# Attention further ahead of its product, factor tails on VectorE, factors made in place, borders reordered

## The chip, the cores and the metric

The kernel runs on one core of a Trainium2 chip. The metric is the device time of one execution in microseconds; runs are told by their median. The engines are TensorE (PE; its weight loads are PEld), VectorE (DVE), ScalarE (ACT), GpSimd (POOL) and SyncE (SP), which here issues every DMA. TensorE's clock has two levels, 1.2 and 2.4 GHz; the profile gives the granted share.

## The reference

Pooled attention and two MLPs on 8 x 576 = 4608 tokens, in float32. The weights come in as 64-bit floats.

```
k_p, v_p = means over 8 neighbours of k, v          # 72 keys a head; 8 batches, 8 heads, 64 dims
scores = (q @ k_p^T) / sqrt(64);  attn = exp(scores - max);  attn /= sum(attn) + 1e-9
x  = attn @ v_p                                     # as 4608 x 512
x1 = silu(x @ w_in)  @ w_out                        # 512 -> 2048 -> 512
h  = x1 @ w_in2;  out = (h * clip(h + 3, 0, 6) / 6) @ w_out2
```

## The kernel before, in words

Every float32 matmul outside the attention is made of three products of halves that TensorE reads at full rate (`F32R`): a *head*, which ScalarE rounds by a copy, and a *tail*, the rest, which another engine gets by a subtraction. The last three of the four big products also use a seven-product form of 2 x 2 blocks: seven sums of weight blocks (the *factors*, `k` = 0 to 6) and seven sums of operand blocks.

The work has four stages, each of nine groups of 512 tokens (`g`), four tiles of 128 tokens (`t`) in a group.

- *Hidden stage* (L863-939): `h_mm` makes one of sixteen slices `f` of a group's hidden values, 12 matmuls of 512 columns; a slot is `(g, f)`, 144 in all. Beside them runs the attention of the next group's tiles, by the table of `stages(g)`: `scores` into two `ps_a` banks; "soft" (`below_max` on VectorE, `exps` on ScalarE); `norm`; a transposition, in the first group on TensorE (`probs_T`), later on VectorE in 32 x 32 blocks (`vector_T`), which go to DRAM and come back in the right order (L475, L479); `weighted`, the product with v five (first group) or six slots after the scores; and `split_x`. `silu` of a slot is issued in the next one. The first group also converts the sixteen slices of w_in (`split_a`, `split_b`).
- Beside it, *factor jobs* (`run_job`) convert w_out and, for 5 of 8 pairs, w_in2: scale on ScalarE (L163), three bit operations on VectorE (L169-L176), sums of blocks on GpSimd (`combine`, L195), a head on ScalarE (`half_head`, L187) and a tail on GpSimd (`half_tail`, L191) for each of seven factors; the two are stored to DRAM (`ws`) and loaded again when the factor is wanted (`load_factor`).
- *Wide stage* (`block_stage(0, ...)`): 63 blocks (g, k) of 48 matmuls of 256 columns. Its operands are split by `split_g` (L678 on ScalarE, L679 on VectorE) one block ahead. After each block `run_steps(2)` does two steps of the last three w_in2 pairs.
- *Product stage* (L1115-1177): 252 slots of 12 matmuls of 256 columns, with gates behind them and one step a slot of the w_out2 pairs. Its operands come from x1 by `x_sum` (GpSimd), `x_head` (ScalarE) and `x_tail`.
- *Last stage* (`block_stage(1, ...)`): again 63 blocks of 48.

All instructions are issued in the order of the program (`manual_schedule`); each engine, and SP's queue of DMAs, takes its own in that order and waits at its head. DMA issues that need a result are put into `later` and issued at the top of the next slot. Tags name buffers: a tile waits until the last use of the tile that held its tag is over.

Of the kernel before, what the change touches and what calls it, by code (L numbers as in the profile page):

```python
# [10 lines left out]
F32 = mybir.dt.float32  # L11
# [14 lines left out]
def kernel(  # L26
# [154 lines left out]
    def half_b(mag, dst):  # L181

        half_tail(mag, half_head(mag), dst)

    def half_head(mag):
        t = prep_tile("out", [P, 2, HW], F32R)
# [27 lines left out]
    def pair_steps(p, piece):  # L214
# [12 lines left out]
        def head(k, key):  # L227
            def run():
                t[k] = half_head(m[key])
            return run  # L230

        def tail(k, key):
            return lambda: half_tail(m[key], t.pop(k), ws[piece][d][k][:, j])
# [13 lines left out]
    def pair_jobs(p, piece, rest):  # L247
# [4 lines left out]
        def out(k, key):  # L252
            return lambda: half_b(m[key], ws[piece][d][k][:, j])
# [22 lines left out]
    def load_factor(m, d, k, tag):  # L276
        t = wts.tile([P, 2, 2, HW], F32R, tag=tag, name="wst")
        nc.sync.dma_start(out=t.bitcast(F32), in_=ws[m][d][k])
# [76 lines left out]
    def load_q(t, tag=None):  # L355
        qt = staging(tag or f"o{10 + t % 2}", DM)
# [70 lines left out]

    def den_of(t):
# [4 lines left out]
    def norm(t, summed=0):  # L433
# [3 lines left out]
        nc.vector.tensor_reduce(out=den[:, :n], in_=pr[:, :n], op=ALU.add, axis=AX.X)  # L437
# [6 lines left out]
    def probs_T(t, tags=A, tag=None, warm=0):  # L444
        pr = p_t.pop(t)
        pT = staging(tag or f"o{12 + t % 2}", H * P)[:SP]
# [14 lines left out]
    def vector_T(t):  # L461
# [4 lines left out]
        bT = staging(f"o{14 + t % 2}", NB * H * Q).rearrange("p (j h q) -> p j h q", j=NB, h=H)  # L466
        pT = staging(f"o{12 + t % 2}", H * P)[:SP].rearrange("p (i h q) -> p i h q", h=H, q=Q)
# [117 lines left out]
    def x_sum(i):  # L585
        b11, b12, b21, b22 = x_blocks()
        if i == 1:
            combine(ALU.subtract, b11, b12, b11)
        elif i == 2:
            combine(ALU.subtract, b11, b22, b11)  # L590
        elif i == 3:
            combine(ALU.subtract, b12, b22, b12)
        elif i == 5:
            combine(ALU.subtract, b21, b21, b11)
# [16 lines left out]
    def make_x(g, i):  # L611

        x_sum(i)
# [46 lines left out]
    LAST = (0, 1, 4, 2, 5, 6, 3)  # L660
# [62 lines left out]
    def stages(g):  # L723
        d = [[] for _ in range(NF)]
        if g + 1 < NG:
            for i in range(TPG):
                t = TPG * (g + 1) + i
                s = (3, 5, 7, 9)[i] if g == 0 else (0, 2, 5, 8)[i]
                d[s].append(("scores", t))
                d[s + 1].append(("soft", t))  # L730
                d[s + 2].append(("norm", t))
                if g == 0:
                    d[s + 3].append(("probs", t))
                else:
                    d[s + 2].append(("turn", t))
                w = s + 5 if g == 0 else s + 6
                d[w].append(("weighted", t))
                d[w + 1].append(("split", t))
        return d

    with tc.manual_schedule():
# [93 lines left out]
        kv_jobs = [(b, j) for b in range(2, B) for j in range(NPAIR)]  # L835
        kv_wait = []
        BUSY = (2, 10)
# [3 lines left out]
        w_need = [(d, k) for k in LAST for d in range(ND)]  # L841
        w_tags = [f"o{i}" for i in range(12)] + [f"i{i}" for i in range(NF)]
# [20 lines left out]
        for g in range(NG):  # L863
            todo = stages(g)
            if g == NG - 1:
                while jobs or jobs_b:
                    run_job()
                    load_halves()
                early.close()
                open_ring()  # L870
            for f in range(NF):
# [6 lines left out]
                while later:  # L878
                    later.pop(0)()
                ps = h_mm(g, f)  # L880
                for what, t in todo[f]:
# [6 lines left out]
                if late_silu:  # L888
                    silu(*late_silu.pop())
                late_silu.append((g, f, ps))  # L890
                for what, t in todo[f]:
                    if what == "split":
                        split_x(t, pv.pop(t))
# [3 lines left out]
                elif g < NG - 1 and f not in BUSY:  # L897
                    run_job()
                for what, t in todo[f]:
                    if what == "soft":  # L900
                        new_pr(t)
                        below_max(t, 0)
                        below_max(t, 1)
                        exps(t, 0)
                        exps(t, 1)
                    elif what == "norm":
                        norm(t)
# [4 lines left out]
                if n < 3:  # L912
                    for j in ((0, 1), (2,), (3,))[n]:
# [3 lines left out]
                if f % 2 == 1:  # L917
                    for b, j in kv_wait:
                        pool_k(b, j, nc.gpsimd)
                        pool_v(b, j)  # L920
                    kv_wait = []
# [317 lines left out]
```

## Time and profile before

| | |
|---|---|
| median of 3 runs | 1668.45 us (1665.39 to 1670.14) |
| the profiled execution | 1662.0 us, of which the span, first to last instruction, is 1660.2 |
| PE, PEld | 1534.5 us busy (92%), 1449.6 (87%) |
| DVE, ACT, POOL | 1264.3 (76%), 737.1 (44%), 530.7 (32%) |
| mean granted clock | 0.967 |
| DMA | 350.56 MB, 211 GB/s |

Busy shares are means over stages that differ. In a row of the timeline the bracket is the idle time of the engine just before it and what ended it; in a list of groups the numbers behind the bar are busy us, the mean ns of one, and idle time.

### The profile page before, as it was taken

The page shows a single profiled execution, that of the slowest core. Times are in us where ns is not written, and L with a number is a line of the kernel's source. Part 1 is how long each engine was busy: PE and PEld are TensorE (multiplying, and loading weights), DVE is VectorE, ACT ScalarE, POOL GpSimd, SP SyncE. Part 2 cuts the span into 40 slices and gives each one's busy share as a digit, 9 for nine tenths or more (in the row PEclk, how much of TensorE's full clock was granted, in tenths as well). Part 3 has the DMA queues.
Part 4 walks back from the last instruction along what each step waited for, and adds up shares of the span by engine and source line. Part 5 has one row for each costly group of instructions (what it writes and reads, how often), then busy time and mean ns, then how long its engine had stood idle before and what let it go on. Part 6 is the DMA issues. An engine that isn't in the chain of part 4 may idle for free.

```text
span 1660.2 us, 30941 instructions
## 1 busy us (share of the span) xinstructions
PE 1534.5 (92%) x11870; PEld 1449.6 (87%) x11870; DVE 1264.3 (76%) x1674; ACT 737.1 (44%) x1241; POOL 530.7 (32%) x590
## 2 busy tenths in 40 slices
PE   7579888898889979999999979999999999999999
PEld 6468777776768869999999979999999899999998
DVE  7867688677787429999977758778776687887776
ACT  5343333333334224444433446777676543344333
POOL 5744545545543002221300036766665000000000
PEclk9789999999999998999999989999999999999999
DMA  9327777867876995554544966656567974444441
GB/s 326 108 66 231 249 235 256 274 221 242 280 244 230 338 358 176 170 184 154 172 146 145 340 252 210 223 211 204 210 215 255 358 274 130 128 151 133 154 149 45
DMA packets 188276, 350.56 MB, mean 211 GB/s; under 512 B 17504, under 2 KB 90080, under 8 KB 188128
## 3 DMA queue, kind: packets, MB, share of 16 engines
q1 hardware_dynamic: 188128, 348.59, 61.7%
q8 instruction: 93, 1.52, 0.4%
q14 instruction: 55, 0.45, 0.1%
HBM read 199.10 MB, written 149.42 MB: 210 GB/s over the span
## 4 chain that ended last, share of the span: by engine, by line
PE 65%; DVE 12%; DMA 11%; issue 4%; POOL 3%; ACT 3%; SPq 1%; DVEq 0%; ACTq 0%; POOLq 0%
PE pl L708 20%; PE pl L692 19%; PE px L630 10%; PE hps L528 6%; PE pz L630 5%; PE py L630 3%; DMA ws<-hout 2%; DMA bl<-stage 2%; DMA wst<-ws 2%; DMA g<-g 2%; DMA stage<-in_k_dram 2%; DVE hmag L176 1%; DVE g L542 1%; DVE hmag L172 1%; DVE hmag L169 1%
## 5 line engine op out<-in xcount | busy, mean ns | idle before, releaser
L528 PE MATMUL hps<-x,whl 128*128 128x512 f32 x1728 | 411.0, 397 | 7.4 <-POOL whl L138 2.8
L528 PEld LDWEIGHTS hps<-x,whl 128*128 128x128 f32 x1728 | 336.6, 198 | 64.4 <-DVE g L542 4.6
L678 ACT ACTIVATE gs<-gr 128x1024 fp32r<-128x1024 f32 x252 | 253.7, 1054 | 260.0 <-issue 104.2
L692 PE MATMUL pl<-gs,wst 128*128 128x256 f32 x3024 | 341.6, 276 | 14.2 <-ACT gs L678 13.7
L692 PEld LDWEIGHTS pl<-gs,wst 128*128 128x128 f32 x3024 | 340.9, 193 | 14.9 <-ACT gs L678 13.9
L679 DVE TENSOR_TENSOR gs<-gr,gs 128x1024 fp32r<-128x1024 f32 x252 | 303.4, 1246 | 54.4 <-ACT gs L678 54.1
L708 PE MATMUL pl<-wst,gs 128*128 128x256 f32 x3024 | 339.8, 276 | 3.3 <-ACT gs L678 2.5
L708 PEld LDWEIGHTS pl<-wst,gs 128*128 128x128 f32 x3024 | 339.5, 193 | 3.7 <-ACT gs L678 2.7
L191 POOL TENSOR_TENSOR hout<-hmag,hout 128x256 fp32r<-128x256 f32 x168 | 149.2, 895 | 417.5 <-ACT hout L187 393.2
L630 PE MATMUL px<-xst,wst 128*128 128x256 f32 x1728 | 208.2, 277 | 11.0 <-ACT c L1148 9.8
L630 PEld LDWEIGHTS px<-xst,wst 128*128 128x128 f32 x1728 | 201.4, 194 | 12.0 <-ACT c L1148 10.2
L542 DVE SCALAR_TENSOR_TENSOR g<-g,hps 128x512 f32<-128x512 f32 x144 | 96.3, 677 | 105.4 <-ACT g L541 101.4
L671 DVE TENSOR_TENSOR gr<-gr 128x1024 f32<-128x1024 f32 x144 | 176.5, 1267 | 0.0
L541 ACT ACTIVATE g<-hps 128x512 f32<-128x512 f32 x144 | 83.8, 588 | 79.5 <-PE hps L528 61.5
L630 PE MATMUL pz<-xst,wst 128*128 128x256 f32 x864 | 109.8, 276 | 2.6 <-POOL xst L607 2.5
L187 ACT ACTIVATE hout<-hmag 128x256 fp32r<-128x256 f32 x168 | 68.1, 411 | 94.2 <-POOL hmag L195 68.7
L607 POOL TENSOR_TENSOR xst<-xr,xst 128x512 fp32r<-128x512 f32 x56 | 76.8, 1371 | 93.5 <-ACT xst L602 88.7
L630 PEld LDWEIGHTS pz<-xst,wst 128*128 128x128 f32 x864 | 102.8, 192 | 3.8 <-POOL xst L607 3.3
L195 POOL TENSOR_TENSOR hmag<-hmag 128x256 f32<-128x256 f32 x96 | 92.1, 963 | 15.9 <-DVE hmag L176 12.7
L413 ACT ACTIVATE pr<-pr 128x288 f32<-128x288 f32 x64 | 28.1, 442 | 153.5 <-DVE pr L406 153.5
L195 POOL TENSOR_TENSOR xr<-xr 128x512 f32<-128x512 f32 x36 | 48.6, 1350 | 128.2 <-DVE xst L607 124.9
L169 DVE TENSOR_SCALAR hmag<-hmag 128x256 uint32<-128x256 uint32 x96 | 52.6, 548 | 40.3 <-ACT hmag L163 39.2
(81 smaller groups left out, 1533.1 us busy)
## 6 DMA issues: line engine op xcount, KB each, us to landing
gr<-g SPq DMA_DIRECT2D x144, 512.0 KB
ws<-hout SPq DMA_DIRECT2D x168, 256.0 KB
wst<-ws SPq DMA_DIRECT2D x84, 512.0 KB
g<-g SPq DMA_DIRECT2D x144, 256.0 KB
g<-go SPq DMA_DIRECT2D x144, 256.0 KB
hraw<-in_moe_w_out_dram SPq DMA_DIRECT2D x64, 256.0 KB
bl<-stage SPq DMA_DIRECT2D x28, 384.0 KB
stage<-in_k_dram SPq DMA_DIRECT2D x32, 288.0 KB
```

The lines of the kernel that those rows point to most:

```text
L191: nc.gpsimd.tensor_tensor(out=t[:, 1], in0=mag, in1=t[:, 0].bitcast(F32), op=ALU.subtract)
L195: nc.gpsimd.tensor_tensor(out=out, in0=a, in1=b, op=op)
L528: nc.tensor.matmul(ps, w[:, c, :], shuffled(x[:, c, :]), start=(c == 0 and n == 0), stop=(c == NKC - 1 and n == 2),)
L541: nc.scalar.activation(in_two(t), dealt(ps), AF.Tanh)
L542: nc.vector.scalar_tensor_tensor(out=in_two(t), in0=in_two(t), scalar=1.0, in1=dealt(ps), op0=ALU.add, op1=ALU.mult)
L607: (eng or nc.gpsimd).tensor_tensor(out=t[:, 1], in0=x_source(i), in1=t[:, 0].bitcast(F32), op=ALU.subtract)
L630: nc.tensor.matmul(ps[:, j * HW:(j + 1) * HW], w[:, j, a, c, :], shuffled(x[:, b, c, :]), start=(first and j == 0 and n == 0 and c == 0), ...
L671: nc.vector.tensor_tensor(out=to, in0=a, in1=b, op=ALU.subtract)
L678: nc.scalar.activation(t[:, dd, 0], src, AF.Copy)
L679: nc.vector.tensor_tensor(out=t[:, dd, 1], in0=src, in1=t[:, dd, 0].bitcast(F32), op=ALU.subtract)
L692: nc.tensor.matmul(ps[:, c * HW:(c + 1) * HW], w[:, b, c * P:(c + 1) * P], shuffled(t[:, dd, a, i]), start=(dd == 0 and c == 0 and i == 0 ...
L708: nc.tensor.matmul(ps[:, c * HW:(c + 1) * HW], t[:, dd, a, i, c * P:(c + 1) * P], shuffled(w[:, b]), start=(dd == 0 and c == 0 and i == 0 ...
```

## The change

- *Attention.* A tile's scores come five slots (group 1), seven (group 2) or ten (from group 3) ahead of its weighted product, by a table over all slots (`todo`, `start`). `all_exps` takes the maxima of all eight heads and then one exponential per head on ScalarE, straight from the scores' banks, which also gives the sums, so that `norm` sums nothing. q has buffers of its own; transposed probabilities have four. k and v are loaded 16 slots ahead of the first scores that read them and pooled three slots later.
- *Order in a slot.* `silu`, `split_x` and the exponentials are issued ahead of the slot's matmuls and jobs. Jobs run in the slots of a group that are not 0, 3, 6 or 13, and in the even slots of the last group.
- *Tails.* `split_b` and `half_tail` subtract on VectorE instead of GpSimd.
- *In place.* Eight of the 28 factors of w_out (`k` = 0 and 1) are made in the buffers in which the wide stage reads them (`direct`, tags o0 to o7), without a store and a load. The other twenty are loaded at another pace, the last after the first raw weights of the wide stage's steps.
- *Borders.* The wide stage's steps begin at its fifth block; the product stage's at its third column (`e > 1`), two in some slots. `x_sum` of the first operands goes to VectorE, operands 5 and 6 are made in the first five product slots, and `split_g(1, 0, 0)` is issued in the last column of products.

```diff
-        nc.gpsimd.tensor_tensor(out=t[:, 1, :], in0=mag, in1=t[:, 0, :].bitcast(F32), op=ALU.subtract)
+        nc.vector.tensor_tensor(out=t[:, 1, :], in0=mag, in1=t[:, 0, :].bitcast(F32), op=ALU.subtract)
...
+    def half_head(mag, m, d, k, j):
+        if (m, d, k) in direct:
+            if j == 0:
+                load_factor(m, d, k, direct[m, d, k], fill=False)
+            t = w_st[m, d, k][:, j]
+        else:
+            t = prep_tile("out", [P, 2, HW], F32R)
         nc.scalar.activation(t[:, 0], mag, AF.Copy)
         return t
 
-    def half_tail(mag, t, dst):
-        nc.gpsimd.tensor_tensor(out=t[:, 1], in0=mag, in1=t[:, 0].bitcast(F32), op=ALU.subtract)
-        later.append(lambda: nc.sync.dma_start(out=dst, in_=t.bitcast(F32)))
+    def half_tail(mag, t, m, d, k, j):
+        nc.vector.tensor_tensor(out=t[:, 1], in0=mag, in1=t[:, 0].bitcast(F32), op=ALU.subtract)
+        if (m, d, k) not in direct:
+            later.append(lambda: nc.sync.dma_start(out=ws[m][d][k][:, j], in_=t.bitcast(F32)))
...
+    direct = {(2, d, k): f"o{ND * i + d}" for i, k in enumerate(LAST[:2]) for d in range(ND)}
...
+    def all_exps(t):
+
+        mx = att.tile([P, H, 1], F32, tag="mxa", name="mxa")
+        for a in range(2):
+            nc.vector.tensor_reduce(
+                out=mx[:, a * NPAIR:(a + 1) * NPAIR], in_=s_t[t][a], op=ALU.max, axis=AX.X
+            )
+        nc.vector.tensor_scalar(out=mx, in0=mx, scalar1=-ESCALE, scalar2=None, op0=ALU.mult)
+        for h in range(H):
+            a, i = divmod(h, NPAIR)
+            nc.scalar.activation(
+                p_t[t][:, a, i], s_t[t][a][:, i], AF.Exp, scale=ESCALE, bias=mx[:, h],
+                accum_out=den_of(t)[:, h],
+            )
+        s_t.pop(t)
...
+        if g == 1:
+            w, back = (7, 9, 11, 13)[i], 5
+        elif g == 2:
+            w, back = NF + (6, 9, 11, 14)[i], 7
+        else:
+            w, back = NF * (g - 1) + (4, 7, 10, 13)[i], 10
+        s = start[t] = w - back
+        jobs = [(s, "scores"), (s + 1, "soft"), (w, "weighted"), (w + 1, "split")]
+        if g == 1:
+            jobs += [(s + 3, "norm"), (s + 4, "probs")]
+        else:
+            jobs += [(s + 3, "norm"), (s + 3, "turn")]
...
-                elif g < NG - 1 and f not in BUSY:
+                elif f % 2 == 0 if g == NG - 1 else f not in REST:
                     run_job()
...
         load_halves()
+        while w_need:
+            next_wide(1)
...
-            run_steps(2)
+            if g or k in LAST[4:]:
+                run_steps(2)
...
-                x_sum(1)
+                x_sum(1, nc.vector)
...
-        make_x(0, 5)
-        make_x(0, 6)
...
+            if e == 0 and pos < 5:
+                x_job(*(("s", 0, 5), ("h", 0, 5), ("t", 0, 5), ("h", 0, 6), ("t", 0, 6))[pos])
...
-            if e < n_all - ND:
-                run_steps(1)
+            if 1 < e < n_all - ND:
+                run_steps(1 + (e % ND == 0 and pos < 3))
+            if (e, pos) == (n_all - 1, 4):
+                split_g(1, 0, 0)
```

## Rows read from the trace of the kernel before

**Rows 1.** Windows by stage: busy us of each engine (instructions), clock, DMA share, GB/s

```profile
29.60:131.40 101.80, 68.64 (x345) 55.67 (x346) 72.99 (x97) 42.07 (x74) 61.79 (x65) 0.82 0.40 130
131.40:558.90 427.50, 377.63 (x2090) 317.03 (x2089) 328.52 (x604) 150.03 (x339) 201.85 (x283) 0.95 0.75 246
558.90:600.30 41.40, 41.40 (x194) 36.25 (x192) 13.18 (x18) 11.34 (x18) 0.00 (x0) 1.00 1.00 386
600.30:656.00 55.70, 41.55 (x343) 41.06 (x342) 35.98 (x39) 18.54 (x25) 8.61 (x6) 0.85 0.63 226
656.00:862.00 206.00, 205.96 (x1844) 205.77 (x1843) 186.68 (x187) 93.32 (x116) 39.01 (x27) 1.00 0.53 174
956.00:982.00 26.00, 16.20 (x122) 15.82 (x121) 10.09 (x18) 8.39 (x18) 2.94 (x3) 0.80 0.66 250
982.00:1313.00 331.00, 327.17 (x2905) 325.25 (x2904) 250.05 (x331) 225.14 (x418) 196.85 (x174) 1.00 0.66 230
1313.00:1329.00 16.00, 12.69 (x96) 12.50 (x97) 12.96 (x14) 7.56 (x9) 0.00 (x0) 0.89 0.95 355
```

**Rows 2.** Timeline: start, us, engine, line; unbroken hidden slots, scores, weighted product

```profile
320.78 1.14 PE L389 MATMUL aps<-kbd,stage 128*128 128x144 f32 x8
...
555.14 1.09 PE L493 MATMUL aps<-stage,vp 72*64 72x128 f32 x16
...
556.16 44.30 PE L528 MATMUL hps<-x,whl 128*128 128x512 f32 x204
```

**Rows 3.** Waits of TensorE, 131.4 to 558.9: us in total, times, longest

```profile
PE aps L493 <- DMA stage<-bl: 31.5, 15, 4.8
PE aps L389 <- DVE pr L406: 6.6, 10, 2.1
```

**Rows 4.** Waits of TensorE, 29.6 to 131.4

```profile
PE aps L389 <- DMA stage<-in_q_dram: 8.6, 1, 8.6
```

**Rows 5.** Timeline: one tile's store of transposes and its weighted product

```profile
303.88 0.50 SPq L475 DMA_DIRECT2D bl<-stage  x1
...
312.78 1.09 PE L493 MATMUL aps<-stage,vp 72*64 72x128 f32 x16 [2.71 <-DMA stage<-bl]
```

**Rows 6.** Groups of VectorE's instructions, 131.4 to 558.9

```profile
L176 DVE SCALAR_TENSOR_TENSOR hmag<-hraw,hmag 128x256 uint32<-128x256 uint32 x52 | 46.6, 897 | 1.8
L172 DVE SCALAR_TENSOR_TENSOR hmag<-hraw,hmag 128x256 uint32<-128x256 uint32 x52 | 33.6, 646 | 1.8
...
L406 DVE TENSOR_TENSOR pr<-aps,mx 128x288 f32<-128x288 f32 x56 | 25.6, 458 | 1.9
...
L437 DVE TENSOR_REDUCE den<-pr 128x8 f32<-128x576 f32 x28 | 20.8, 743 | 0.0
```

**Rows 7.** Groups of ScalarE's instructions, 131.4 to 558.9

```profile
L187 ACT ACTIVATE hout<-hmag 128x256 fp32r<-128x256 f32 x91 | 37.6, 413 | 82.9 <-POOL hmag L195 63.0 <-DMA ws<-hout 19.8
```

**Rows 8.** Groups of GpSimd's instructions, 131.4 to 558.9

```profile
L195 POOL TENSOR_TENSOR hmag<-hmag 128x256 f32<-128x256 f32 x52 | 44.6, 858 | 1.3
```

**Rows 9.** Timeline: the first and the last of four exponentials per head (first group)

```profile
18.73 0.31 ACT L422 ACTIVATE stage<-aps,mx 128x72 f32<-128x72 f32 x1
...
19.62 0.32 ACT L422 ACTIVATE stage<-aps,mx 128x72 f32<-128x72 f32 x1
```

**Rows 10.** Timeline: border from the hidden to the wide stage

```profile
622.29 0.43 ACT L163 ACTIVATE hmag<-hraw 128x256 f32<-128x256 f32 x1 [19.30 <-DMA hraw<-in_moe_w_in_dram]
...
624.87 0.80 PE L692 MATMUL pl<-gs,wst 128*128 128x256 f32 x2 [13.69 <-ACT gs L678]
```

**Rows 11.** Timeline: border from the wide to the product stage

```profile
969.90 0.43 ACT L163 ACTIVATE hmag<-hraw 128x256 f32<-128x256 f32 x1 [9.47 <-DMA hraw<-in_moe_w_out_dram]
...
971.49 5.23 PE L630 MATMUL px<-xst,wst 128*128 128x256 f32 x24 [8.06 <-ACT c L1148]
```

**Rows 12.** Waits of TensorE, 977.9 to 1313

```profile
PE pz L630 <- POOL xst L607: 2.5, 3, 0.9
```

**Rows 13.** Timeline: one long bit operation on VectorE in the hidden stage

```profile
324.82 1.95 DVE L176 SCALAR_TENSOR_TENSOR hmag<-hraw,hmag 128x256 uint32<-128x256 uint32 x1
```

More of the change, by code (lines that the diff above doesn't have):

```diff
@@ L355, in load_q @@
     def load_q(t, tag=None):
-        qt = staging(tag or f"o{10 + t % 2}", DM)
+        qt = staging(tag, DM) if tag else att.tile([P, DM], F32, tag="q", name="qT")
         nc.sync.dma_start(out=qt, in_=q[t])
@@ L436, in norm @@
         n = H - summed * NPAIR
-        nc.vector.tensor_reduce(out=den[:, :n], in_=pr[:, :n], op=ALU.add, axis=AX.X)
+        if n:
+            nc.vector.tensor_reduce(out=den[:, :n], in_=pr[:, :n], op=ALU.add, axis=AX.X)
         nc.vector.tensor_scalar(
@@ L583, in x_blocks, with x_sum @@
         return [x_raw[a, b] for a in range(2) for b in range(2)]
-    def x_sum(i):
+    def x_sum(i, eng=None):
         b11, b12, b21, b22 = x_blocks()
[L587 to L594, printed above, removed]
+        if i in (1, 2, 3, 5):
+            to, a, b = {1: (b11, b12, b11), 2: (b11, b22, b11), 3: (b12, b22, b12), 5: (b21, b21, b11)}[i]
+            (eng or nc.gpsimd).tensor_tensor(out=to, in0=a, in1=b, op=ALU.subtract)
     def x_source(i):
@@ L720 @@
             first_tile.setdefault(b, t)
[L723 to L739, printed above, removed]
+    todo = {}
+    start = {}
+    for t in range(TPG, NTILE):
+        g, i = divmod(t, TPG)
+        if g == 1:
[10 more added lines that the diff above has]
+            jobs += [(s + 3, "norm"), (s + 3, "turn")]
+        for n, what in jobs:
+            todo.setdefault(n, []).append((what, t))
+    kv_in = {}
+    for b in range(2, B):
+        for j in range(NPAIR):
+            kv_in[start[first_tile[b]] - 16 + 4 * j] = (b, j)
     with tc.manual_schedule():
@@ L833 @@
         load_ahead(6)
-        kv_jobs = [(b, j) for b in range(2, B) for j in range(NPAIR)]
-        kv_wait = []
-        BUSY = (2, 10)
+        REST = (0, 3, 6, 13)
         jobs = list(factor_jobs())
@@ L840 @@
         jobs_b = []
-        w_need = [(d, k) for k in LAST for d in range(ND)]
-        w_tags = [f"o{i}" for i in range(12)] + [f"i{i}" for i in range(NF)]
+        w_need = [(d, k) for k in LAST[2:] for d in range(ND)]
+        w_tags = [f"o{i}" for i in range(8, 12)] + [f"i{i}" for i in range(NF)]
         def next_wide(n):
@@ L879 @@
                     later.pop(0)()
+                if late_silu:
+                    silu(*late_silu.pop())
+                for what, t in todo.get(n, ()):
+                    if what == "split":
+                        split_x(t, pv.pop(t))
+                    elif what == "soft":
+                        new_pr(t)
+                        all_exps(t)
                 ps = h_mm(g, f)
-                for what, t in todo[f]:
+                late_silu.append((g, f, ps))
+                for what, t in todo.get(n, ()):
                     if what == "scores":
@@ L887 @@
                         pv[t] = weighted(t, A if g == 0 else [(ps_y, f"y{2 + t % 2}")])
[L888 to L893, printed above, removed]
                 if g == 0:
@@ L896 @@
                     conv_a(1, f % 2)
-                elif g < NG - 1 and f not in BUSY:
+                elif f % 2 == 0 if g == NG - 1 else f not in REST:
                     run_job()
[L899 to L907, printed above, removed]
+                for what, t in todo.get(n, ()):
+                    if what == "norm":
+                        norm(t, 2)
                     elif what == "turn":
@@ L911 @@
                         probs_T(t, [(ps_y, "y2"), (ps_y, "y3")])
-                if n < 3:
-                    for j in ((0, 1), (2,), (3,))[n]:
+                if n < 2:
+                    for j in (2 * n, 2 * n + 1):
                         pool_k(1, j)
@@ L916 @@
                     pool_v(1, n - 1)
[L917 to L921, printed above, removed]
-                    if kv_jobs and f % 4 == 1 and TPG * (g + 1) + f // 4 + 5 >= first_tile[kv_jobs[0][0]]:
-                        b, j = kv_jobs.pop(0)
-                        load_k(b, j)
-                        load_v(b, j)
-                        kv_wait.append((b, j))
-                if g == NG - 2 and f >= NF - 4:
-                    next_wide(2)
+                if n - 3 in kv_in:
+                    pool_k(*kv_in[n - 3], nc.gpsimd)
+                    pool_v(*kv_in[n - 3])
+                if n in kv_in:
+                    load_k(*kv_in[n])
+                    load_v(*kv_in[n])
+                if g == NG - 2 and f in (8, 10):
+                    next_wide(1)
                 if g == NG - 1:
@@ L940 @@
         silu(*late_silu.pop())
+        while jobs or jobs_b:
+            load_halves()
+            run_job()
         while later:
             later.pop(0)()
-        while w_need:
-            next_wide(1)
         coming = {}
```

37 lines of the change are left out of this document (16 added, 21 removed).

## The prediction

> **What bounds the kernel now.** I read the busy windows by stage first [rows 1]. TensorE is busy without a break in the wide stage (656 to 862 us: 205.96 of 206) and nearly so in the product stage (327 of 331), so nothing taken from another engine can shorten those insides: 1844 matmuls in 206 us are 111.7 ns each, which makes 5.36 us a block of 48 and 1.34 us a slot of 12. Time is lost in five places: the first hidden group (29.6 to 131.4), the hidden stage after it (131.4 to 558.9, clock 0.95), and three borders: hidden to wide, wide to products, products to last.
>
> The hidden stage has a clean floor. In its last group 204 matmuls, 17 slots, run in 44.30 us, 2.61 us a slot; a tile's scores take 1.14 and its weighted product 1.09 [rows 2]. So 112 slots and 28 tiles cost 292 + 62 = 354 us against 427.5: 73 lost. The list of waits names the largest: TensorE's weighted product waits 31.5 us for the transposed probabilities that come back through DRAM, and the scores wait 6.6 for VectorE to free their banks [rows 3]. A mean clock of 0.95 says that 10% of the 427.5 us ran at 1.2 GHz instead of 2.4, about 43 us, which costs half of it, 21; these slow stretches follow idle time. The first group waits for the q load [rows 4] and has VectorE busy 73 of 101.8 us [rows 1].
>
> At the borders: 600.3 to 656 holds 343 matmuls, 38.3 us of work in 55.7, so 17.4 lost; 956 to 982 holds 122, 13.6 in 26, so 12.4 lost; 1313 to 1329 holds 96, 10.7 in 16, so 5.3 lost [rows 1].
>
> **The change part by part.**
>
> *Attention ten slots ahead.* One tile's way from the store of its transposes to its weighted product took 312.78 - 303.88 = 8.9 us, of which TensorE stood 2.71 [rows 5]. Transposes now follow the scores by three slots and the product by ten: seven slots of about 3.16 us (354 / 112), 22 us. In group two the distance is four slots, 12.6 us, still over 8.9. The 31.5 go. What is late next: the scores' banks. Scores now come three slots apart (two in groups one and two), and their bank is free only after eight exponentials. Four such exponentials start 0.30 us apart (18.73 to 19.62) [rows 9], so eight take 2.4 us and, with two maxima ahead on VectorE, end some 5 us after the scores; three slots are 9.5. I let the 6.6 go too. The clock's 21 shrinks with the gaps; I take 17. Sum 55 of 73. Bounds: 20 (part of the DRAM wait, the rest turned into new waits) to 73 (the floor).
>
> *Who pays.* VectorE loses 56 subtractions and 28 sums, 25.6 + 20.8 = 46.4 us [rows 6], and gains 28 small scalings (between nothing and L406's 0.46 us each; I take 0.2, so 6) and 84 of the stage's tails, moved from GpSimd. No row shows a 128x256 subtraction there; the nearest are L172 and L176, of the same shape with two SBUF inputs, at 646 and 897 ns [rows 6]. I take 0.65, so 55. 328.5 - 46 + 6 + 55 = 343 us of VectorE in a stage of 372: 92%, under TensorE, with little room; that is why I leave 18 of the 73. Below it, without GpSimd in the way, a tail costs at the least what a column of L406 does: 458 ns for 288 columns, 0.41 for 256. ScalarE goes from 150 us [rows 1] by at most 28 x 2.4 = 67 to 217 of 372 us. The exponentials wait for VectorE's maxima, and behind them in ScalarE's order stand the slot's job and the next slot's tanh; that tanh frees a bank which TensorE wants three slots, some 9 us, later. Silu and split move ahead of that wait.
>
> A rule that speaks against the tails: the Trainium skill, "SBUF — State Buffer", section "Who interferes with whom", says that a VectorE instruction with two SBUF inputs and a GpSimd instruction that reads SBUF lock each other out for the whole of the one that came first. The trace agrees: L406, with one of its large inputs in PSUM, has a steady 458 ns, while L176 averages 897 [rows 6]. By the rule each tail could wait out a whole GpSimd combination, and the time would be rival A's, 1620; by the rows it is the sum's.
>
> *First group.* 11 to 15 wide tails (128x512, twice L172's columns: 0.8 to 1.3 us) join VectorE, +12; 8 subtractions and 4 sums go, -7 at rows 6's means. The stage cannot be shorter than VectorE's 73 + 5 = 78. The q load gets a buffer of its own and is no longer queued behind a k load, so its 8.6 us [rows 4] shrink, but VectorE works through that wait and would hold TensorE next. The maxima now come ahead of the weight conversion in VectorE's order. I take 8; bounds 24 won to 5 lost.
>
> *Eight factors in place.* 16 stores of 256 KB and 8 loads of 512 KB go; 4.2 MB at the 386 GB/s of the last group [rows 1] are 11 us of DMA, beside TensorE's work and worth nothing by themselves, but they are in the queue ahead of what the border waits for.
>
> *Costed at nothing.* The k and v loads, now sixteen slots ahead of the scores that read them and pooled three slots later, lie beside GpSimd's idle half (202 busy of 427.5); eight jobs that move into the last group find VectorE busy there 13 of 41.4 us [rows 1]; the four buffers of transposed probabilities use tags that nothing else holds then. If that cover goes, each is a wait of the size of the 6.6 in rows 3.
>
> *Border hidden to wide.* TensorE's 13.69 us wait is for ScalarE, and ScalarE stood 19.30 us before a scaling (L163) whose raw weights lay behind twelve factor loads [rows 10]. Now the raw weights are loaded ahead of the remaining factors, the first four blocks run no such step, and the first two blocks' factors need no load. Both the wait and its slow clock go. Ten factors are left to load, the first wanted four blocks, 21 us, on: 5.2 MB at 386 GB/s are 13.6 us. I take 16 of 17.4; bounds 8 to 17.4.
>
> *Inside the wide stage.* 21 tails at 0.65 bring VectorE's 186.7 of 206 [rows 1] to 200: I put 1 us of loss; bounds 0 to 8.
>
> *Border wide to products.* The same pattern: ScalarE stood 9.47 us before L163, TensorE 8.06 before ScalarE's copy [rows 11]. The steps now start at the third output column, 14 slots on; the sums go to VectorE; two of the seven operands are made in the first five slots, on GpSimd, for slots 7 on. I take 10.5 of 12.4; bounds 6 to 12.4.
>
> *Inside the products.* 327 of 331 busy; the 2.5 us in which TensorE waited for GpSimd's tails of x [rows 12] mostly go with GpSimd's load. VectorE's 250 of 331 [rows 1] gains 56 x 0.65 = 36. I take 2; bounds 4 lost to 6 won.
>
> *Border to the last stage.* The first split starts four slots, 5.4 us, earlier, between the last gates on ScalarE and VectorE, which it delays. I take 3 of 5.3; bounds 5.3 won to 2 lost.
>
> Sum: 8 + 55 + 16 - 1 + 10.5 + 2 + 3 = 93.5. The profiled execution took 1662.0 us for a span of 1660.2; 1662.0 - 93.5 = 1568.5. The median of the runs, 1668.45, stands 6.45 above that execution: **1575**.
>
> **The rivals.**
>
> A. VectorE becomes the bound of the hidden stage. Each tail waits for a whole combination on GpSimd: 0.86 [rows 8] + 0.41 = 1.27 us. Hidden stage 288 (328.5 - 46 + 6) + 84 x 1.27 = 395, with 5 for jams 400: 27 won instead of 55. Wide stage 186.7 + 27 = 213.6, 8 lost. Products none won, first group none. 1662 - 48.5 + 6.45 = 1620. For it: L176's 897. Against: GpSimd gives up the tails and is busy less than its 202 of 427.5.
>
> B. ScalarE's queue passes waits on. It stood 63 us in the hidden stage for GpSimd's combinations ahead of a head [rows 7]; exponentials and tanh now stand behind the same waits with less time to spare. If half of the 63 reaches TensorE, 30 of the 55 are lost: 1605. Against: hardly any of it reached TensorE before [rows 3].
>
> C. The borders find a next wait: the DMA runs at a share of 1.00 before the first [rows 1], and raw weights and factors still use one queue. If 17 of the 29.5 stay: 1592.
>
> D. Slower. One mechanism: the price of a tail on VectorE. At the 1.95 us that one L176 took [rows 13] the hidden stage is 288 + 164 = 452, 25 longer; the wide stage 186.7 + 41 = 228, 22 longer; the products 250 + 109 = 359, 28 longer; less the borders' 29.5: 1714. It decides from 1.67 us a tail: there 161 tails cost what all of it wins. Against: a mean of 0.65 to 0.90 in the same stretch, with GpSimd busier than it will be.
>
> E. The products still wait for DRAM although they come later, because the queue that issues the stores is itself late. 31.5 and 17 stay: 1623. Against: 8.9 us needed, 22 given.
>
> **How the numbers follow.** Forecast 0.58, A 0.10, B 0.15, C 0.12, D 0.03, E 0.02. What a measurement of this kernel can tell from no change is 0.3%, 5 us. Every case but D is faster by far more; I keep 0.02 for several falling together: faster 0.95, within 0.02, slower 0.03. The range takes the forecast with its bounds (the hidden stage at its floor and 17 won in the first group give 1548), B and C, and stops short of A: 1548 to 1612.
>
> **What would show it.** Right: no row in which a weighted product waits for transposes; 112 slots in 360 to 385 us; no wait over 2 us at 600 and 960; the subtraction on VectorE at 0.4 to 0.7 us. Wrong: a clock under 0.97 in the hidden stage; VectorE busy over 95% of it (A); scores waiting for ScalarE's exponentials (B); a wide or product stage in which TensorE's share falls under 98% (D).

## The result, and the profile after

The changed kernel takes 1588.13 us (median of four runs, 1586.87 to 1592.09) against 1667.77 (four runs beside it, 1665.39 to 1670.14): a ratio of 0.9527, with a 95% interval of 0.9504 to 0.9549. The forecast was 1575, within a range of 1548 to 1612. The profiled execution took 1589.21 us, its span is 1586.9 (before 1660.2), its mean clock 0.983 (0.967).

By stage, in us of the two spans, with what the prediction's steps add up to:

| stage | before | after | difference | predicted |
|---|---|---|---|---|
| start | 29.6 | 30.9 | +1.3 | 0 |
| first hidden group | 101.8 | 95.3 | -6.5 | -8 |
| hidden groups 1 to 7 | 427.5 | 391.3 | -36.2 | -55 |
| last hidden group | 41.4 | 41.4 | 0 | 0 |
| border 1 and wide stage | 355.6 | 337.7 | -17.9 | -15 |
| border 2 and products | 359.6 | 348.4 | -11.2 | -12.5 |
| border 3 and last stage | 344.7 | 341.9 | -2.8 | -3 |
| sum | 1660.2 | 1586.9 | -73.3 | -93.5 |

These are the windows of the kernel after that answer to [rows 1], with the same columns:

```profile
30.90:126.20 95.30, 68.02 (x352) 54.22 (x353) 71.18 (x106) 50.34 (x131) 46.37 (x50) 0.84 0.42 133
126.20:517.50 391.30, 364.31 (x2084) 308.40 (x2083) 286.67 (x618) 189.35 (x717) 126.32 (x187) 0.97 0.78 253
517.50:558.90 41.40, 41.40 (x193) 36.25 (x192) 21.32 (x38) 15.51 (x30) 2.96 (x5) 1.00 1.01 379
558.90:614.60 55.70, 55.70 (x500) 55.70 (x499) 49.05 (x54) 26.32 (x34) 1.47 (x2) 1.00 0.72 260
614.60:820.00 205.40, 205.40 (x1842) 205.40 (x1841) 181.76 (x208) 91.39 (x114) 13.21 (x10) 1.00 0.53 175
896.60:922.60 26.00, 26.00 (x236) 26.00 (x235) 15.13 (x21) 15.77 (x29) 8.46 (x7) 1.00 0.82 309
922.60:1245.00 322.40, 315.47 (x2793) 312.94 (x2792) 266.49 (x385) 220.03 (x409) 147.12 (x117) 1.00 0.66 231
1245.00:1261.00 16.00, 16.00 (x146) 16.00 (x145) 15.78 (x17) 8.03 (x10) 0.00 (x0) 1.00 0.96 362
```

Rows four, six and eight are the borders: where TensorE was busy 41.55 of 55.7, 16.20 of 26 and 12.69 of 16 us it now has no gap at all. The wide stage is one unbroken run. The second row is where time is left: 391.3 us against a floor of 354. In the products TensorE is busy 315.47 of 322.40.

TensorE's waits in hidden groups 1 to 7, answering to [rows 3] (us in total, times, longest):

```profile
PE aps L399 <- DMA qT<-in_q_dram: 11.4, 6, 4.2
PE hps L555 <- ACT x L536: 4.8, 1, 4.8
PE aps L520 <- DMA stage<-bl: 4.5, 2, 2.6
PE aps L399 <- POOL kbd L331: 3.2, 2, 2.2
PE aps L399 <- ACT pr L448: 1.5, 3, 0.6
PE hps L555 <- DVE g L569: 1.4, 2, 0.8
```

The 31.5 us for transposes that come back through DRAM are down to 4.5, the 6.6 for the scores' banks (VectorE) to 1.5 (now ScalarE's exponentials). New at the top is the wait for q. Together these rows are 26.8 us. The mean clock of 0.97 says that some 6% of 391.3 us ran at 1.2 GHz instead of 2.4, which costs half of it, 12. So 39 us stand against the 37 above the floor: within the rounding of the clock, nothing else is lost there.

What ScalarE and VectorE do in the same stretch answers to [rows 6, 7]. ScalarE's waits:

```profile
ACT pr L448 <- DVE mxa L445: 124.2, 28, 8.6
ACT g L568 <- PE hps L555: 33.1, 24, 3.8
ACT hout L192 <- POOL hmag L201: 28.9, 18, 4.0
```

GpSimd's longest wait:

```profile
POOL hmag L201 <- DVE hout L196: 173.7, 29, 19.4
```

VectorE's groups (busy us, mean ns, then idle time before them and its releasers):

```profile
L172 DVE SCALAR_TENSOR_TENSOR hmag<-hraw,hmag 128x256 uint32<-128x256 uint32 x48 | 31.8, 663 | 1.8
...
L196 DVE TENSOR_TENSOR hout<-hmag,hout 128x256 fp32r<-128x256 f32 x66 | 30.2, 458 | 63.0 <-ACT hout L192 59.3 <-DMA g<-g 3.5
...
L176 DVE SCALAR_TENSOR_TENSOR hmag<-hraw,hmag 128x256 uint32<-128x256 uint32 x48 | 24.4, 509 | 1.6
...
L196 DVE TENSOR_TENSOR wst<-hmag,wst 128x256 fp32r<-128x256 f32 x16 | 9.1, 570 | 17.8 <-ACT wst L192 17.8
```

A tail costs VectorE 458 to 570 ns, and VectorE is busy 286.67 of 391.3 us, 73%. It waits 77 us for ScalarE's heads (59.3 + 17.8), while ScalarE waits 124 us for VectorE's maxima, and neither is full. Whether each engine's order holds the other up is what experiments 9 and 10 ask.

### The profile page after: what moved, and what is told of

Its sections match the earlier page's. It is cut to its first block, busy times and chain, and to the rows that moved or that the text cites. A ratio compares the mean times of both kernels' runs of the same rounds, so it can differ in the third digit from the quotient of the medians.

```text
span 1586.9 us, 31188 instructions
## 1 busy us (share of the span) xinstructions
PE 1514.5 (95%) x11870; PEld 1433.9 (90%) x11870; DVE 1244.2 (78%) x1795; ACT 788.9 (50%) x1689; POOL 361.2 (23%) x405
## 2 busy tenths in 40 slices
DMA packets 184820, 342.17 MB, mean 216 GB/s; under 512 B 17120, under 2 KB 89696, under 8 KB 184672
## 4 chain that ended last, share of the span: by engine, by line
PE 71%; DVE 12%; DMA 9%; ACT 4%; issue 2%; POOL 1%; SPq 1%; ACTq 0%; DVEq 0%; POOLq 0%
PE pl L729 21%; PE pl L713 21%; PE hps L555 11%; PE px L652 9%; PE pz L652 4%; PE py L652 2%; DMA bl<-stage 2%; ACT pr L448 2%; DVE g L569 2%; DVE hmag L172 1%; DMA wraw<-in_moe_w_in_dram 1%; DMA g<-g 1%; DVE go L1098 1%; DMA hraw<-in_moe_w_out_dram 1%; DVE hmag L169 1%
## 5 line engine op out<-in xcount | busy, mean ns | idle before, releaser
L555 PE MATMUL hps<-x,whl 128*128 128x512 f32 x1728 | 402.9, 392 | 9.6 <-ACT x L536 5.6
L555 PEld LDWEIGHTS hps<-x,whl 128*128 128x128 f32 x1728 | 331.7, 195 | 63.5 <-ACT x L536 6.3
L700 DVE TENSOR_TENSOR gs<-gr,gs 128x1024 fp32r<-128x1024 f32 x252 | 298.0, 1224 | 36.8 <-ACT gs L699 36.2
L201 POOL TENSOR_TENSOR hmag<-hmag 128x256 f32<-128x256 f32 x96 | 82.2, 860 | 455.2 <-DVE hout L196 390.0
L692 DVE TENSOR_TENSOR gr<-gr 128x1024 f32<-128x1024 f32 x144 | 169.5, 1218 | 0.0
L448 ACT ACTIVATE pr<-aps,mxa 128x72 f32<-128x72 f32 x256 | 78.1, 330 | 139.1 <-DVE mxa L445 139.1
L196 DVE TENSOR_TENSOR hout<-hmag,hout 128x256 fp32r<-128x256 f32 x152 | 83.4, 556 | 64.2 <-ACT hout L192 60.4
L192 ACT ACTIVATE hout<-hmag 128x256 fp32r<-128x256 f32 x152 | 62.7, 420 | 56.6 <-POOL hmag L201 37.0
L399 PE MATMUL aps<-kbd,qT 128*128 128x144 f32 (+1 forms) x288 | 44.5, 311 | 33.0 <-DMA qT<-in_q_dram 16.0
L399 PEld LDWEIGHTS aps<-kbd,qT 128*128 128x128 f32 (+1 forms) x288 | 36.6, 188 | 41.5 <-ACT pr L448 13.0
```

The lines of the kernel that those rows point to most:

```text
L196: nc.vector.tensor_tensor(out=t[:, 1], in0=mag, in1=t[:, 0].bitcast(F32), op=ALU.subtract)
L201: nc.gpsimd.tensor_tensor(out=out, in0=a, in1=b, op=op)
L448: nc.scalar.activation(p_t[t][:, a, i], s_t[t][a][:, i], AF.Exp, scale=ESCALE, bias=mx[:, h], accum_out=den_of(t)[:, h],)
L555: nc.tensor.matmul(ps, w[:, c, :], shuffled(x[:, c, :]), start=(c == 0 and n == 0), stop=(c == NKC - 1 and n == 2),)
L692: nc.vector.tensor_tensor(out=to, in0=a, in1=b, op=ALU.subtract)
L700: nc.vector.tensor_tensor(out=t[:, dd, 1], in0=src, in1=t[:, dd, 0].bitcast(F32), op=ALU.subtract)
```

## The experiments

All ratios are to the kernel before, timed beside each version. The diffs are against the changed kernel. Times of single stages come from one traced execution of each version.

**1. Is SP's queue what makes q late?** SP stands before the loads of the transposes until the stores have landed, and the q loads are behind them. The load is issued two or three slots later.

```diff
+        def fetch():
...
+        fetches.append((slot_now[0] + (2 if t < 3 * TPG else 3), fetch))
```

> The changed kernel, with the read-back of the transposed probabilities issued two slots (group 2: one slot) after their store. Theory 1, SP's queue: in the hidden stage SP stands 114.6 us for the stores to land, 28 times, and the q loads behind it come late. Then that wait falls under 30 us, TensorE's 11.4 us of waits for q in groups 1 to 7 under 3, these groups go from 391 to 370-378 us, and the time to 1568-1578. Rival, the DMA itself: a q load takes 5 us from issue to landing at a DMA share of 0.78, so q stays late by 8 us or more and the time stays at 1583-1590.

Measured: 1587.41 us (1582.42 to 1588.05), ratio 0.9516 (0.9497 to 0.9535): no change. SP's waits in the hidden stage, first of the changed kernel, then of this one:

```profile
SPq L506 <- DMA bl<-stage: 114.6, 28, 6.6
SPq L153 <- DVE hmag L176: 24.9, 22, 4.0
```

```profile
SPq L153 <- DVE hmag L176: 105.7, 40, 6.8
...
SPq L511 <- DMA bl<-stage: 7.5, 5, 3.2
```

The wait that was taken away stands one place on in the queue: the load of the next raw weights waits for the buffer that VectorE has yet to read. TensorE's wait for q stays, 8.7 us. So SP's wait for the stores is not by itself what costs the time. Whether SP's queue as a whole makes q late this run does not show, since SP stood as long as before, 201 us against 197 in all.

**2. Tails back on GpSimd.**

```diff
-        nc.vector.tensor_tensor(out=t[:, 1], in0=mag, in1=t[:, 0].bitcast(F32), op=ALU.subtract)
+        nc.gpsimd.tensor_tensor(out=t[:, 1], in0=mag, in1=t[:, 0].bitcast(F32), op=ALU.subtract)
```

(and the same in `split_b`)

> The changed kernel, with all tails (split_b and half_tail) on GpSimd again. Theory: the move of the tails is worth something, since a tail takes VectorE 0.46 to 0.56 us and GpSimd 0.75, and the heads wait for GpSimd's sums of blocks. Then ScalarE's wait for GpSimd's sums in groups 1 to 7 goes from 29 back to 50 us or more and the time to 1594-1606. Rival: VectorE is what fills the hidden and the product stage, so that tails taken from it win: 1575-1583, and the products lose 7 us where they now lose 10.

Measured: 1624.43 us (1623.49 to 1626.3), ratio 0.9747 (0.973 to 0.9764): 36 us of the change's 80 are gone, 29 of them in hidden groups 1 to 7 (420.2). TensorE's waits in the hidden stage:

```profile
PE aps L399 <- POOL kbd L331: 20.3, 5, 4.9
PE aps L399 <- ACT pr L448: 9.7, 7, 3.7
```

and GpSimd's:

```profile
POOL hout L196 <- ACT hout L192: 152.1, 54, 11.9
POOL wst L196 <- ACT wst L192: 48.7, 15, 10.3
```

GpSimd is busy only 188 of 420 us. But its tails stand 201 us waiting for ScalarE's heads, and the pooling of k is queued behind them: it comes late for the scores. That a tail was moved is worth the waits that went with it, not its own duration. One rival stands: of the four loads of a batch's k only the first comes sixteen slots ahead of the scores; the others come 12, 8 and 4 ahead (`start[...] - 16 + 4 * j`), so that the last is pooled one slot ahead of its use. Whether an earlier pooling would have made GpSimd's queue harmless was not tried.

**3. Exponentials as before**: subtractions and sums of halves on VectorE.

```diff
-                        all_exps(t)
+                        below_max(t, 0)
+                        below_max(t, 1)
+                        exps(t, 0)
+                        exps(t, 1)
...
-                        norm(t, 2)
+                        norm(t)
```

> The changed kernel, with the exponentials as before: VectorE subtracts the maxima and sums the rows, ScalarE does two wide exponentials a tile. VectorE gains some 40 us in groups 1 to 7 (287 to 325 of 391) and ScalarE loses 90. Theory: VectorE's queue is the one that makes others late, so this costs: 1594-1604. Rival: the exponentials on ScalarE are the new late step (the first group's scores wait 7 us for them), so this wins or costs nothing: 1578-1589.

Measured: 1585.34 us (1583.24 to 1588.17), ratio 0.9511 (0.9495 to 0.9528): no difference. The 41 us of VectorE's time that this part saves in groups 1 to 7 (286.7 against 328.0 busy) are not on the path; ScalarE's wait for VectorE is 142.6 us in this form and 124.2 in the other.

**4. Six slots instead of ten** (six in group 2 too).

```diff
-            w, back = NF * (g - 1) + (4, 7, 10, 13)[i], 10
+            w, back = NF * (g - 1) + (4, 7, 10, 13)[i], 6
...
-            jobs += [(s + 3, "norm"), (s + 3, "turn")]
+            jobs += [(s + 2, "norm"), (s + 2, "turn")]
```

> The changed kernel, with the distance from scores to weighted product at six slots from group 2 on, transposes two slots after the scores, as before; all else of the change stays. Theory: the distance is what won the hidden stage; the products wait 25 us or more for the transposes again, groups 2 to 7 have slow clock again, and the time is 1612-1632. Rival: the other edits (order in a slot, spacing of three slots, tails, exponentials) won it, and the time is under 1600.

Measured: 1614.92 us (1607.07 to 1617.17), ratio 0.9679 (0.965 to 0.9708): 27 us. TensorE in the hidden stage:

```profile
PE aps L520 <- DMA stage<-bl: 28.3, 12, 4.2
```

The wait of [rows 3] is back nearly whole, and the clock of the stage falls from 0.97 to 0.94.

**5. Steps at the borders at once.** They begin with the stage's first block and first column, and all factors are loaded ahead of the raw weights.

```diff
+        while w_need:
+            next_wide(1)
         load_halves()
-        while w_need:
-            next_wide(1)
...
-            if g or k in LAST[4:]:
-                run_steps(2)
+            run_steps(2)
...
-            if 1 < e < n_all - ND:
+            if e < n_all - ND:
```

> The changed kernel, with the order of the borders' steps as before: the wide stage runs its steps from the first block, the remaining factors are loaded ahead of the first raw weights, the product stage runs its steps from its first slot. Theory: ScalarE's in-order wait for raw weights behind factor loads is what cost the first border; then the wide stage goes from 337.7 back to 350-356 us, the product stage from 348 to 354-359, and the time to 1606-1617. Rival: the factors made in place have already taken the queue off the border, and the product border's loss was the operands 5 and 6; then both stages stay within 4 us and the time is under 1595.

Measured: 1619.82 us (1617.73 to 1620.31), ratio 0.9719 (0.969 to 0.9747): 32 us, 16.1 in the wide stage and 15.3 in the products. TensorE from 545 to 960 us:

```profile
PE pl L713 <- ACT gs L699: 12.2, 1, 12.2
PE px L652 <- ACT c L1162: 10.9, 1, 10.9
```

and ScalarE at the first border:

```profile
ACT hmag L163 <- DMA hraw<-in_moe_w_in_dram: 17.7, 2, 17.4
```

The chain of [rows 10, 11] as the prediction reads it: raw weights behind factors, ScalarE before them, TensorE behind ScalarE. At the first border the run undoes the order of the steps and of the loads together, so it does not divide the gain between them.

**6. No factor in place.** All 28 are stored and loaded.

```diff
-    direct = {(2, d, k): f"o{ND * i + d}" for i, k in enumerate(LAST[:2]) for d in range(ND)}
+    direct = {}
...
-        w_need = [(d, k) for k in LAST[2:] for d in range(ND)]
+        w_need = [(d, k) for k in LAST for d in range(ND)]
```

> The changed kernel, with all 28 factors of w_out stored and loaded again (eight more loads, ten in the last hidden group but one), ten left at the border as now. Theory: making eight in place is worth nothing by itself, since the order of the steps keeps the border clear: 1584-1593, wide stage 337-340 us. Rival: the saved DMA of 8 MB is what keeps the queue and the hidden stage on time: 1598 or more.

Measured: 1598.26 us (1597.32 to 1603.54), ratio 0.9599 (0.9561 to 0.9637): 10 us slower. The border and the wide stage are unchanged (337.7); of the traced 10 us, 8 lie in hidden groups 2 to 8, where ScalarE waits for stores to empty the buffers of heads:

```profile
ACT hout L192 <- DMA ws<-hout: 11.3, 4, 4.5
```

(0.6 us in the changed kernel). How these waits reach TensorE is not shown.

**7. q two tiles ahead.**

```diff
-                        if t + 1 < NTILE:
-                            load_q(t + 1)
+                        if t + 2 < NTILE:
+                            load_q(t + 2)
```

> The changed kernel, with q loaded two tiles ahead into three buffers instead of one ahead into two. Theory: lead is what the q loads lack; TensorE's waits for q (11.4 us in groups 1 to 7, 4.6 in group 0) fall under 2 us, groups 1 to 7 go from 391 to 373-381 and the time to 1566-1578. Rival: another late operand (pooled k, a bank) stands right behind q, as it did when the read-backs were moved, and the time stays at 1583-1590.

Measured: 1587.77 us (1585.21 to 1588.83), ratio 0.9526 (0.9497 to 0.9555). TensorE's largest waits in the hidden stage:

```profile
PE aps L399 <- ACT pr L448: 7.8, 10, 1.8
PE aps L399 <- POOL kbd L331: 6.2, 2, 3.2
```

The largest row of the list is gone and the time is the same: the scores wait for the next thing. Groups 1 to 7 are 3.9 us shorter in the trace.

**8. All operands earlier**: experiments 1 and 7 together, group 2's scores nine slots ahead, k and v earlier, and raw weights later, at most two buffers of them filled ahead instead of three.

```diff
-            w, back = NF + (6, 9, 11, 14)[i], 7
+            w, back = NF + (4, 7, 10, 13)[i], 9
...
-                    load_halves()
+                    load_halves(2)
```

> The kernel of the q loads two ahead, with more lead for all that was late in the hidden stage: read-backs two slots after their store, raw weights loaded one buffer later so that SP does not stand for VectorE, k and v three slots earlier, group 2's attention nine slots ahead instead of seven. Theory: the hidden stage is now held by in-order queues with too little lead and not by any engine's work; groups 1 to 7 reach 360-370 us (floor 354) and the time is 1554-1568. Rival: VectorE (287 of 391 us busy) and its order hold the stage, so that the time stays at 1575 or above.

Measured: 1587.92 us (1585.91 to 1588.73), ratio 0.9528 (0.9499 to 0.9556). In place of the operands:

```profile
PE hps L561 <- DVE g L575: 9.3, 8, 3.1
PE aps L399 <- ACT pr L448: 8.3, 11, 3.3
```

Groups 1 to 7 are 5.3 us shorter (385.9), the first group 4.2 longer (99.5); two tiles of group 2 now have their scores there instead of one.

**9. Tails at the start of the next job**, so that VectorE does not stand for ScalarE.

```diff
-        half_tail(mag, half_head(mag, *to), *to)
+        t = half_head(mag, *to)
+        pending.append(lambda: half_tail(mag, t, *to))
```

> The changed kernel, with the hidden stage's tails on VectorE issued at the start of the next job instead of right behind their heads. In groups 1 to 7 VectorE stood 77 us before tails whose heads were not ready on ScalarE (59.3 + 17.8), while ScalarE stood 124 us before exponentials whose maxima were not ready on VectorE. Theory: these two in-order queues hold each other up, and that is what is left of the hidden stage's loss. Then VectorE's 77 us fall under 40 and groups 1 to 7 go from 391 to 370-381: 1568-1578. Rival: VectorE has time for that waiting and the stage is held by operands that come late one after another: 1583-1590.

Measured: 1591.89 us (1589.5 to 1592.7), ratio 0.9558 (0.954 to 0.9575): not faster. VectorE's longest wait and its wait for heads in groups 1 to 7:

```profile
DVE hmag L169 <- ACT hmag L163: 64.0, 30, 3.4
...
DVE hout L203 <- ACT hout L199: 10.6, 4, 2.7
```

VectorE's 77 us for heads shrink to 11, but it now stands 64 us before L169, for ScalarE's scaling (L163) that opens the next conversion. ScalarE's wait for maxima stays at 123 us: that VectorE's wait for heads held it up is not borne out.

**10. Exponentials behind the slot's job.** The maxima stay where they are; the eight exponentials are issued after the job, and no longer stand ahead of it in ScalarE's order.

```diff
+        mxs[t] = mx
+
+    mxs = {}
+
+    def head_exps(t):
+        mx = mxs.pop(t)
         for h in range(H):
...
-                    if what == "norm":
+                    if what == "soft":
+                        head_exps(t)
+                    elif what == "norm":
```

> The changed kernel, with the maxima where they are and the eight exponentials issued on ScalarE behind the slot's job instead of ahead of it. Theory of the two queues: ScalarE's 124 us of waiting for maxima shrink to under 80, heads come earlier, VectorE's 77 us before tails shrink too, groups 1 to 7 take 373-383 us: 1570-1580. Rival: the banks of the scores, freed later, hold the next scores (1.5 us now) and take it all back: 1584 or more.

Measured: 1571.51 us (1564.12 to 1576.3), ratio 0.9434 (0.9402 to 0.9466): 17 us faster than the changed kernel (some 16 by the ratios). By the spans, 13.5 us are won in the first group (81.8), 5.9 in groups 1 to 7 (385.4), and 2.4 are lost in the products, where experiments 6, 7 and 9, which leave them alone, also lose 1.6. The time lies where the theory put it, but by luck: most of the gain is in the first group, which the theory did not name, and groups 1 to 7 stay above its 373 to 383. ScalarE's waits from 31 to 112 us, first of the changed kernel, then of this one:

```profile
ACT pr L448 <- DVE mxa L445: 15.0, 4, 6.2
ACT whl L137 <- POOL hout L125: 12.9, 8, 4.4
```

```profile
ACT whl L137 <- DVE hout L127: 10.6, 4, 4.6
ACT whl L137 <- POOL hout L125: 8.1, 4, 4.4
ACT stage L487 <- PE aps L486: 6.4, 5, 2.6
```

One of the four waits for maxima in the changed kernel's timeline:

```profile
60.34 0.32 ACT L448 ACTIVATE pr<-aps,mxa 128x72 f32<-128x72 f32 x1 [6.24 <-DVE mxa L445]
```

and VectorE's wait, before the tail of a slice of w_in (L138), for the head (L137) in that kernel:

```profile
DVE whl L138 <- ACT whl L137: 14.0, 5, 3.2
```

This one falls to 0.2 us. In the first group the two engines had waited for each other: ScalarE, with a weight conversion behind the exponentials, for the maxima, and VectorE for that conversion. In groups 1 to 7 the wait for maxima falls from 124.2 to 76.6 us, and little of that reaches TensorE.

**11. Experiments 7, 9 and 10 together**, with k, v and group 2 as early as in experiment 8.

> Tails with the next job, exponentials behind the job, q two tiles ahead, k and v three slots earlier from batch 4 on and group 2 nine slots ahead. Theory of the two queues: with their hold on each other loosened the leads pay too; groups 1 to 7 take 360-370 us of a floor of 354: 1553-1567. Rival: no order of these queues gets the stage under 380 us, since VectorE with its 290 us of work and its latencies is the bound: 1578 or more.

Measured: 1576.49 us (1574.68 to 1579.31), ratio 0.9473 (0.9452 to 0.9495): no better than 10 alone (5 us more, with intervals that overlap). Groups 1 to 7 are the shortest of all, 378.7 us, but the first group takes 92.2 instead of 81.8.

**12. Experiments 7 and 10 together.**

> The exponentials of a slot issued behind that slot's job on ScalarE (1571.5 us by itself), and the q load two tiles ahead as well. With the exponentials moved alone, the scores of the hidden stage still wait 11.9 us for q in four places, the longest row of TensorE's list there. Theory 1 (ScalarE's queue was what took the q load's place as next wait when q alone was moved, 1587.8 us; with that gone the q wait can be won): scores <- q gone, nothing of its size in its place, 1560 to 1565 us. Theory 2 (the wait goes over to the next one in line again, as with q alone; VectorE's maxima and GpSimd set the pace of the hidden stage): 1568 to 1576 us, with waits for the exponentials or for GpSimd in the list.

Measured: 1570.17 us (1564.39 to 1571.22), ratio 0.9422 (0.94 to 0.9444): with experiment 10 the best of the versions, and not to be told from it. TensorE's list in the hidden stage:

```profile
PE aps L399 <- ACT pr L454: 8.7, 12, 1.3
PE aps L399 <- POOL kbd L331: 3.8, 3, 2.1
PE aps L526 <- DMA stage<-bl: 3.4, 2, 1.8
```

The second theory held: q's 11.9 us went, and the exponentials' 8.7 came; groups 1 to 7 are 3.9 us shorter (381.5), and the start is 3.8 longer (34.8 us; it lies between 30.0 and 32.9 in the other versions). The first group keeps experiment 10's gain (81.5), so an earlier q is not what cost experiment 11 its first group; part of it may be the work of group 2 that moves there, as in experiment 8; its other parts were not tried apart.

## Why the prediction came out as it did

The direction and the range held; the middle was 13 us low. The traced sum was 1568.5 and came out at 1589.2, 20.7 above; 7.5 of that went back, by luck, in the step from the profiled execution to the median, since the changed kernel's profiled run stands 1.1 us above its median, where the one before stood 6.45 below. The range held in part because it was drawn wide enough for the rivals B and C: C's 1592 is nearer to the result than the forecast, and its mechanism is not there.

Of the signs of being right, the price of a tail and the borders without waits came true. The 112 slots took 391.3 us, over the 360 to 385, and two weighted products still waited for transposes; the clock of 0.97 stands at the limit that was named.

**The term that was mis-sized** is "Sum 55 of 73", for hidden groups 1 to 7: 36.2. The distance itself did what was worked out: 31.5 became 4.5, and with six slots it is 28.3 again (experiment 4). The rest, 4.5, is two waits in group 2, so "12.6, still over 8.9" was too tight there. What failed is "I let the 6.6 go too": I took the list of waits as terms that can be struck one by one. The banks' wait shrank to 1.5, but q, k and a late split came up in its place (11.4, 3.2 and 4.8), and experiments 7 and 8 show that it goes on so: they strike the largest rows and the time stays. By the windows, TensorE's idle time there fell from 49.9 to 27.0 us, 22.9 where 38.1 were put down, and its busy time by 13.3, where 17 were put down for the clock.

One of the terms costed at nothing rests on a misreading: the k and v loads come sixteen slots ahead of the scores for the first of four only (experiment 2). Pooled k costs TensorE 3.2 us in groups 1 to 7, and 6.2 once q is early (experiment 7).

**Who pays** had the wrong sign. I entered the tails as a cost to VectorE, 55 us covered by slack, and the exponentials per head as what paid for it. Experiment 2 makes the move of the tails worth 36 us in all; experiment 3 makes the exponentials worth nothing. A tail was estimated at 0.65 us and takes 0.46 to 0.57; 343 us of VectorE were forecast, and 286.67 are there, part of the difference because L176 fell from 897 to 509 ns. The prices of experiments 2, 4 and 5 with 6 (36, 27, 32 and 10 us) sum to 105 where the change wins 80: they overlap. The issue of `silu` and `split_x` ahead of the matmuls and the spacing of the jobs were not tried apart. In groups 1 to 7 alone experiments 2 and 4 give back 29 and 23 us of the 36 that were won there.

The Trainium skill, "SBUF — State Buffer", section "Who interferes with whom", has a tail contend with a GpSimd instruction that reads SBUF. The trace agrees where the two meet: this tail ended 0.28 us after the last of three GpSimd instructions.

```profile
290.60 0.45 POOL L348 TENSOR_TENSOR vp<-stage 72x128 f32<-72x128 f32 x1
290.61 2.09 DVE L196 TENSOR_TENSOR wst<-hmag,wst 128x256 fp32r<-128x256 f32 x1 [2.96 <-ACT wst L192]
291.01 1.41 POOL L201 TENSOR_TENSOR hmag<-hmag 128x256 f32<-128x256 f32 x2
```

But in groups 1 to 7 they seldom meet. Counted in the timeline, 62 of the 82 tails began with no GpSimd instruction running and took 0.40 to 0.43 us, the 0.41 that the prediction named as the least; the other 20 averaged 0.67. A combination mostly waits for the tail of its operand (GpSimd's 173.7 us), so the program's own order keeps them apart. That is why rival A's 1.27 us a tail was not paid. The 1.95 us of [rows 13], D's price, began inside a GpSimd instruction too.

**First group**: -6.5 for -8. The reason given against more ("VectorE works through that wait and would hold TensorE next") is not what held it: experiment 10 brings it to 81.8, near the 78 that were worked out as VectorE's bound. The maxima ahead of the conversion, named as a gain, put the exponentials ahead of it on ScalarE too.

**In place**: "worth nothing by themselves" is off by 10 us (experiment 6), and the use named for them, at the border, is not where they help. The sum was half of what went as well: 16 stores and 8 loads are 8.4 MB (350.56 to 342.17), 22 us at 386 GB/s and not 11.

**Borders**: 17.4, 12.4 and 5.3 were all won, where 16, 10.5 and 3 were taken; experiment 5 shows the first two by the chain that was named; no run tried the third. **Inside**: the wide stage lost nothing (1 was put down). In the products 2793 matmuls at 111.7 ns are 312.0 of 322.4 us, 10.4 lost, against 2905 and 324.5 of 331 before, 6.5: about 4 lost where 2 won were forecast. No run looked into that; the trace's longest single wait there, 2.57 us at 942.72, is for ScalarE's copy (L1163), and ScalarE had stood 4.81 us for VectorE (L176) ahead of a head of the steps.

**Rivals.** A falls: VectorE is 73% busy, and a tail costs under half of 1.27. D falls with it. E falls for ten slots; experiment 4 is E at six. C falls: no border lost anything. B is the one that is partly true. ScalarE's queue does pass waits on, but those for the maxima and not for the combinations (63.0 became 28.9), and mostly in the first group. Experiment 10 wins 6 of the 19 us that were missed in groups 1 to 7. The rest of those is open: all of it is waits and slow clock, no engine is full, and no single lead or order that was tried removes it.

## What to carry to other kernels

Before costing a moved instruction by its duration, look at what it waits for and what is queued behind it: the tails took 0.46 to 0.57 us each, but on GpSimd they held the keys behind 201 us of waiting. A row of the list of waits is won only if what comes next in line is earlier by as much; after the first large one, expect the rows to be replaced. Where two engines each wait long for the other and neither is full, try their order before their load: one exchange won 16 us (experiment 10), another nothing (9), and 41 us less load nothing (3).

## What the runs showed of the hardware

By these traces the time of VectorE's bit operation L176, and of GpSimd's combinations, goes by whether one begins inside an instruction of the other engine, and not by how busy that engine is. L176 averaged 897 ns before [rows 6], 509 in the changed kernel and 585 with the tails back on GpSimd. Counted in the timelines of hidden groups 1 to 7, 39 of 52, 9 of 48 and 21 of 48 began inside a GpSimd instruction and averaged 1.04, 0.70 and 0.73 us; all others took 0.42 to 0.52.

It holds the other way round. GpSimd's combinations averaged 858 ns before [rows 8] and 736 in the changed kernel. Before, 22 of 52 took 0.90 to 1.25 us, and each of these began inside L176 or inside the product of probabilities and reciprocal sums (L442), as here:

```profile
312.13 0.83 DVE L176 SCALAR_TENSOR_TENSOR hmag<-hraw,hmag 128x256 uint32<-128x256 uint32 x1
312.64 0.91 POOL L195 TENSOR_TENSOR hmag<-hmag 128x256 f32<-128x256 f32 x1
```

In the changed kernel none of 48 takes over 0.82 us.
